# A dm step moved between two matmul halves, two loads issued later, and a table load moved, in a fused transformer-block backward kernel

## The chip, the cores and the metric

The kernel runs on one core of one Trainium2 chip. The metric is the device time of one execution in microseconds. Before the change it was run five times; the median is 819.18 us, the lowest 818.51, the highest 819.75. One more execution was taken with the hardware profiler.

## The reference

The kernel computes one transformer block and all of its gradients. x is 2048 x 640 in bf16, with 32 heads of 20 columns; the FFN is 1728 wide.

```python
def _A_ref(x, wqkv, wo):                      # linear attention
    qkv = (x @ wqkv) split into q, k, v per head
    phi = lambda t: jnp.where(t > 0, t + 1, jnp.exp(t)) + 1e-6
    pq, pk = phi(q), phi(k)
    kv = jnp.einsum("bhsd,bhse->bhde", pk, v)
    z = jnp.einsum("bhsd->bhd", pk)
    num = jnp.einsum("bhqd,bhde->bhqe", pq, kv)
    den = jnp.einsum("bhqd,bhd->bhq", pq, z)[..., None] + 1e-6
    return merge_heads(num / den) @ wo
def _B_ref(x, w_gate, w_up, w_down):          # SwiGLU
    return (_silu(x @ w_gate) * (x @ w_up)) @ w_down
h = x + _A_ref(_layernorm(x), A_wqkv, A_wo)
h2 = h + _B_ref(_layernorm(h), B_w_gate, B_w_up, B_w_down)
# outputs: h2, and by jax.vjp with grad_out the gradients of
# A_x, A_wqkv, A_wo, B_w_gate, B_w_up, B_w_down
```

## The kernel before

The 2048 rows are cut into 16 tiles of 128 rows (ST = 16), the 640 columns into 5 blocks of 128 (DT = 5). A product with 640 output columns is done as two halves of 320 columns (NCH), each of 5 matmuls, in the two banks of one PSUM buffer. There are four such buffers (`mm`). The stages follow one another on TensorE:

1. **Start and the k and q products** (0 to 55 us). `warm(31)` issues 31 small matmuls of the identity (ps_warm) while x arrives. Then tile 0 is centred on VectorE, transposed on TensorE (ps_t), copied to SBUF, eight more warm matmuls follow, and the products ps_kq begin.
2. **Attention summaries** (55 to 98 us). Y = xn^T pk (ps_y), the block-diagonal KV, and W2 = KV applied to wo (ps_w2t). Five pieces of W2T are written to SBUF by ScalarE, and each is transposed by an SP DMA (L524) into W2, which lies in the tile named wvo. Piece i gives the 128 columns i of W2. `normalise` runs on VectorE, four tiles at a time, and `tr_pqs` transposes its result into pqsT.
3. **dm steps.** `dm_steps` is a generator of 24 steps. One step multiplies dh2T (grad_out transposed) with a part of w_down for two row tiles: 10 matmuls (ps_dm, L396) and a ScalarE copy (L410); for the last eight steps also a store (scr_dm). They need nothing from attention, and `dm(n)` places n of them in other work: four among ps_y, five around W2, and one behind each of tiles 0 to 14 in the next loop.
4. **The attention loop** (98 to 148 us). For tile t: ps_a = pqsT[t] x W2 (10 matmuls in two halves by `mm_row`), VectorE adds x (xr), takes the statistics (mv2), GpSimd forms rstd (L139, L140). Two tiles later h1 is stored by a DMA on ScalarE's queue (scr_h, L554), VectorE writes hn (L555), and an SP DMA transposes it into hnT (L557).
5. **The FFN in four groups of columns** (148 to 456 us; 448, 448, 448, 384). For each pair of tiles TensorE computes pg (gate) and pu (up), 10 matmuls each; ScalarE makes two sigmoids and two copies (L604 to L607); VectorE makes seven products (L613), among them m_s (the product that the down projection's gradient reads) and dd (gradients of gate and up). dd is transposed by SP DMAs into three rotating `stg` tiles (L616) and stored by GpSimd DMAs (scr_dT, L617). After the eight pairs of a group come the weight gradients `dw` (ps_dw, L652). The first of them multiplies dh2 (grad_out itself, the tile shown as dh in the profile) with m_s, taking tiles 14 and 15 last; its results, dwev, are stored by GpSimd DMAs (L656).
6. **The backward pass through FFN, attention and both layer norms, and the output h2** (456 to 816 us).

The order on TensorE, VectorE and SP is written out by hand in stages 2 to 4; in stage 5 only SP's is, and ScalarE's, VectorE's and GpSimd's instructions are placed by a scheduler. DMAs go out on the queues of SP, ScalarE and GpSimd (POOL), each in order: an issue that waits holds up what is queued behind it.

What the change touches: dh2 is loaded in four quarters of four row tiles each (640 KB each) by GpSimd's queue (L563). Its buffer was pqsT's, so the loads can start when the last ps_a is done. The FFN's gate and up weights of a group are one tile `wgu` of two buffers, loaded on SP's queue (L185, L186); groups 0 and 1 are asked for ahead of the loop, the buffer of group 1 being free after the last dm step. `wait_for(on, dmas)` makes each of a list of DMAs wait for one instruction. The sigmoid's function table is loaded (ACT_TABLE_LOAD) where ScalarE first meets a sigmoid, in the first pair of group 0. `t` in the FFN loop steps by two, so t = 2 is the second pair.

Of the kernel before, what the change touches and what calls it, by code (L numbers as in the profile page):

```python
# [8 lines left out]
FP32 = mybir.dt.float32  # L9
BF16 = mybir.dt.bfloat16  # L10
ALU = mybir.AluOpType
ACT = mybir.ActivationFunctionType
# [3 lines left out]
P = 128  # L16
# [4 lines left out]
def kernel(  # L21
# [8 lines left out]
    nc = tc.nc  # L30
# [4 lines left out]
    DT = D // P  # L35
    NCH = [(0, 320), (320, 640)]
# [287 lines left out]
    with tc.manual_schedule(engines={EngineType.PE, EngineType.DVE, EngineType.Activation, EngineType.Pool}):  # L324

        ps = mm("ps_warm")

        def warm(n):
            for _ in range(n):
                nc.tensor.matmul(ps[:, 0, :P], lhsT=ident[:], rhs=ident[:], start=True, stop=True)  # L330

        def copies(t, eng_copy):
            for sl, src in ln1_tr(t):
                c = eng_copy(out=xnT[:, t, sl], in_=src)
                if t == 0 and sl.start == 0:
                    wait_for(c, load_3())

        def copy1(t):
            (nc.vector.tensor_copy if t in BY_V else nc.scalar.copy)(out=xnT[:, t], in_=ln1_tr1(t))

        warm(31)
        ln1_stats(0)
        ln1_centre(0, 0, 3 * P)
        ln1_centre(0, 3 * P, D)
        copies(0, nc.scalar.copy)
        warm(8)
        ln1_stats(1)
        ln1_centre(1)
        kq_mm(0, 0, lambda: copies(1, nc.vector.tensor_copy), PIECES)
        ln1_stats(2)  # L350
        ln1_centre(2)
        kq_mm(1, 0, None, PIECES)
        ln1_stats(3)
        kq_mm(0, 1, lambda: copy1(2), PIECES)
        phi(0, 0)
        ln1_xn(3)
        kq_mm(1, 1)
        for t in range(2, ST):
            if t == 2:
                ln1_stats(4)  # L360
            if t > 3 and t + 3 < ST:
                ln1_stats(t + 3)
            kq_mm(t, 0, (lambda: copy1(t + 1)) if t + 1 < ST else None)
            if t == 2:
                ln1_stats(5)
            if t == 3:
                ln1_stats(6)
            if t == ST - 1:
                phi(0, t - 1, 1)
            kq_mm(t, 1)  # L370
            if t == 3:
                phi(1, 0)
            elif t == ST - 1:
                phi(0, t, 1)
                phi(1, t - 3)
                phi(1, t - 1)
            elif t > 3:
                phi(t % 2, t - 2 - t % 2)
            if t + 2 < ST:
                ln1_xn(t + 2)  # L380
            if ST - NC - 1 <= t < ST - 1:
                ln1_xn(t - ST + NC + 1)
# [34 lines left out]
    def dm(n):  # L417
        for _ in range(n):
            next(dms, None)
# [41 lines left out]
    with tc.manual_schedule(engines={EngineType.PE, EngineType.DVE, EngineType.SP}):  # L461
        yk = strips.tile([P, DT * D + HG * P], BF16, name="yk", tag="S")
        Yt = yk[:, :DT * D].rearrange("p (k n) -> p k n", k=DT)
        KVT = yk[:, DT * D:].rearrange("p (j c) -> p j c", j=HG)
        zs = [wk("zs"), wk("zl")]

        def z_sum():
            ps = mm("ps_z")
            for ci, (n0, n1) in enumerate(NCH):
                for t in range(ST):  # L470
                    q = t % 4 * H
                    nc.tensor.matmul(ps[q:q + H, ci, :320], lhsT=ones[:, :H], rhs=pk[:, t, n0:n1],
                                     start=(t < 4), stop=(t >= ST - 4))
            nc.scalar.copy(out=half(zs[0][:]), in_=row(ps))
            nc.vector.tensor_tensor(out=half(zs[1][:]), in0=row(ps), in1=half(zs[0][:]), op=ALU.subtract)
            nc.vector.memset(KVT, 0.0)

        for i in range(DT):
            ps = mm("ps_y")
            for ci, (n0, n1) in enumerate(NCH):  # L480
                for t in range(ST):
                    nc.tensor.matmul(ps[:, ci, :320], lhsT=xn[:, t, i * P:(i + 1) * P], rhs=pk[:, t, n0:n1],  # L482
                                     start=(t == 0), stop=(t == ST - 1))
                if (i, ci) == (0, 0):
                    z_sum()
            nc.scalar.copy(out=half(Yt[:, i, :]), in_=row(ps))
            if i == 0:
                ps_z = mm("ps_zb")
                mm_row(ps_z, lambda k: ones32[:], lambda k, n0, n1: zs[k][:, n0:n1], 2)
                nc.scalar.copy(out=half(zb[:]), in_=row(ps_z))  # L490
                masks()
            if 0 < i < 4:
                dm(1)
        dm(1)
        for t in (0, 4):
            normalise(t)
            tr_pqs(t)
        for t in range(6):
            load_xr(t)
        nc.sync.dma_start(out=mat_v(scr_Yt), in_=Yt)  # L500
        def kv_blocks(dst, name, lhs, rhs):
            for js in ((0,), (1, 2), (3, 4), (5,)):
                h0, h1 = HC[js[0]]
                ps = mm(name)
                for c, j in enumerate(js):
                    for i in range(DT):
                        nc.tensor.matmul(ps[:, c, :h1 - h0], lhsT=lhs(i, OH[j], OH[j] + P),
                                         rhs=rhs(i, OH[j] + h0, OH[j] + h1), start=(i == 0), stop=(i == DT - 1))
                n = len(js)
                nc.vector.tensor_tensor(out=dst[:, js[0]:js[0] + n, h0:h1], in0=ps[:, :n, :h1 - h0],  # L510
                                        in1=head_mask(js[0], h1 - h0).unsqueeze(1).to_broadcast([P, n, h1 - h0]), op=ALU.mult)

        kv_blocks(KVT, "ps_kvt", lambda i, a, b: wv[:, i, a:b], lambda i, a, b: Yt[:, i, a:b])

        W2T = wv
        W2 = wo6[:, 0:5]
        dm(1)
        for i in range(DT):
            if i % 2 == 0 and i > 0:
                dm(1)  # L520
            ps = mm("ps_w2t")
            mm_heads(ps, lambda j: wo6[:, j, i * P:(i + 1) * P], lambda j, a, b: KVT[:, j, a:b])
            nc.scalar.copy(out=half(W2T[:, i, :]), in_=row(ps))
            nc.sync.dma_start_transpose(out=W2[:, :, i * P:(i + 1) * P], in_=W2T[:, i, :])  # L524
        for t in (8, 12):
            normalise(t)
            tr_pqs(t)
        dm(2)

        hn = big.tile([P, ST, D], BF16, name="hn", tag="B")  # L530
        hnT = big.tile([P, DT, S], BF16, name="hnT", tag="B")
        h1s = {}
        for t in range(ST + 2):
            if t < ST:
                xr = xrs.pop(t)
                ps = mm("ps_a")
                mm_row(ps, lambda i: pqsT[:, i, t * P:(t + 1) * P], lambda i, n0, n1: W2[:, i, n0:n1], DT)
                nc.vector.tensor_tensor(out=half(xr[:]), in0=row(ps), in1=half(xr[:]), op=ALU.add)
                mv = small.tile([P, 4, 2], FP32, name="mv2", tag="mv2")
                ln_stats(xr[:], mv[:, 0, :])  # L540
                ln_rstd(mv, rstd2, t, 1)
                h1s[t] = (xr, mv)
                dm(1)
            if t > 2:
                load_xr(t + 3)
            u = t - 2
            if u < 0:
                continue
            if u == 0:
                nc.sync.dma_start(out=scr_KVT.rearrange("(j p) c -> p j c", p=P), in_=KVT)  # L550
            if u == 2:
                nc.sync.dma_start(out=mat_v(scr_W2T), in_=W2T)
            h1, mv = h1s.pop(u)
            nc.scalar.dma_start(out=scr_h1_v[:, u, :], in_=h1[:])  # L554
            nc.vector.tensor_scalar(out=hn[:, u, :], in0=h1[:], scalar1=mv[:, 0, 0:1],  # L555
                                    scalar2=rstd2[:, u:u + 1], op0=ALU.subtract, op1=ALU.mult)
            nc.sync.dma_start_transpose(out=hnT[:, :, u * P:(u + 1) * P], in_=hn[:, u, :])  # L557


    with tc.manual_schedule(engines={EngineType.SP}):  # L560
        dh2 = big.tile([P, ST, D], BF16, name="dh2", tag="B")
        for c in range(4):
            nc.gpsimd.dma_start(out=dh2[:, c * 4:(c + 1) * 4, :], in_=go_v[:, c * 4:(c + 1) * 4, :])  # L563

        wgT = {}
        wgu = {0: load_wgu(0), 1: load_wgu(1)}

        def tr_wgT(g):
            k0, r0 = divmod(KO[g], 14)
# [4 lines left out]
        for g in range(4):  # L574
# [4 lines left out]
            for t in range(0, ST, 2):  # L579
# [21 lines left out]
                nsg = fw("nsg")[:, :, :w]  # L601
                u = fw("u")[:, :, :w]

                nc.scalar.activation(out=dg, in_=pg[:, :, :w], func=ACT.Sigmoid)  # L604
                nc.scalar.activation(out=nsg, in_=pg[:, :, :w], func=ACT.Sigmoid, scale=-1.0)
                nc.scalar.copy(out=m, in_=pg[:, :, :w])
                nc.scalar.copy(out=u, in_=pu[:, :, :w])  # L607
# [426 lines left out]
```

## Time and profile before

| | |
|---|---|
| median of five runs | 819.18 us (818.51 to 819.75) |
| profiled execution | 820.71 us, its span 818.70 us |
| TensorE matmuls | 811.5 us busy, 5534 instructions |
| VectorE, ScalarE, GpSimd | 443.0, 288.2 and 192.4 us busy |
| TensorE clock granted | 1.00 in the mean |
| mean DMA traffic | 194 GB/s, 158.61 MB moved |
| the dm group ps_dm | 47.0 us, 240 matmuls of 448 or 384 columns |

The span runs from the first to the last instruction of the profile; the 2.01 us between it and the execution's own time lie around it. PE stands for TensorE's matmuls, PEld for its weight loads, DVE for VectorE, ACT for ScalarE, POOL for GpSimd; SPq, ACTq and POOLq are DMA issues. A line of a timeline gives the start in us, the length in us, engine, source line, operation, output and inputs, and how many instructions were merged; in brackets stands how long the engine had been idle and what ended that. Lengths of merged matmuls include the drain of the last one, so that starts are the better measure of pitch. A line of the waits gives who waited for whom: us in total, times, longest.

### The profile page before, as it was taken

What the parts mean: (1) busy time and instruction counts of PE and PEld (TensorE: products, weight loads), DVE (VectorE), ACT (ScalarE), POOL (GpSimd) and SP (SyncE); (2) the same over time, 40 slices, a digit from 0 to 9 for tenths busy, and PEclk for the clock granted to TensorE, in tenths of its full rate; (3) what the DMA queues carried; (4) which work ended last, traced back from release to release, by engine and by line L of the source; (5) the groups of instructions that cost most, each with busy time, mean ns of one, the idle gap of its engine ahead of it and who ended that gap; (6) DMA issues with size and microseconds to landing.
All of it is one profiled execution on the core that took longest, in us unless ns stands there. A gap on an engine that the chain in (4) does not pass through costs nothing.

```text
span 818.7 us, 13969 instructions
## 1 busy us (share of the span) xinstructions
PE 811.5 (99%) x5534; PEld 521.9 (64%) x5534; DVE 443.0 (54%) x849; ACT 288.2 (35%) x405; POOL 192.4 (23%) x350
## 2 busy tenths in 40 slices
PE   8999999999999999999999999999999999999998
PEld 6776566545555555555566677777777777777675
DVE  7878787791077018810660147787793366631212
ACT  6982422770184126500741122322322133322010
POOL 3420022222312312221124511211220111112330
PEclk9999999999999999999999999999999999999999
DMA  9994699998559996995498757976498999999952
GB/s 302 189 357 88 166 197 273 263 226 191 159 130 196 218 219 145 199 247 115 101 241 170 261 134 218 221 203 180 111 240 169 161 173 178 169 199 263 242 165 72
DMA packets 278321, 158.61 MB, mean 194 GB/s; under 512 B 235052, under 2 KB 264877, under 8 KB 278256
## 3 DMA queue, kind: packets, MB, share of 16 engines
q1 hardware_dynamic: 251696, 82.12, 52.9%
q0 software_dynamic: 17744, 64.45, 26.0%
q10 hardware_dynamic: 8816, 11.16, 4.7%
q8 instruction: 43, 0.70, 0.4%
q14 instruction: 22, 0.18, 0.1%
HBM read 47.68 MB, written 53.66 MB: 124 GB/s over the span
## 4 chain that ended last, share of the span: by engine, by line
PE 94%; DVE 4%; DMA 1%; ACT 1%; issue 0%; ACTq 0%; DVEq 0%
PE ps_dw L652 21%; PE ps_dhn L109 14%; PE ps_dxn L904 8%; PE ps_o L966 7%; PE ps_kq L302 5%; PE ps_dwqk L109 5%; PE pu L588 5%; PE pg L583 5%; PE ps_dm L396 5%; PE ps_y L482 3%; PE ps_dp L109 3%; PE ps_dk L109 3%; PE ps_gt L711 3%; PE ps_a L109 3%; PE pdm L396 2%; DVE m_s L613 1%
## 5 line engine op out<-in xcount | busy, mean ns | idle before, releaser
L109 PE MATMUL ps_dhn<-wgT,cols 128*128 128x320 bf16 x864 | 119.5, 299 | 0.0
L652 PE MATMUL ps_dw<-dd,hn 128*128 128x448 bf16 (+1 forms) x640 | 118.8, 346 | 0.0
L109 PEld LDWEIGHTS <-cols 128*128 128x128 bf16 x864 | 84.5, 98 | 32.9
L652 PEld LDWEIGHTS <-hn 128*128 128x128 bf16 x640 | 62.6, 98 | 54.2
L654 DVE CAST dwev<-ps_dw 128x896 bf16<-128x896 f32 (+3 forms) x12 | 10.9, 906 | 122.9 <-PE ps_dw L652 122.9
L654 ACT CAST dwev<-ps_dw 128x896 bf16<-128x896 f32 (+1 forms) x20 | 17.6, 878 | 161.9 <-PE ps_dw L652 140.3
L617 POOL DMA_DIRECT2D scr_dT<-stg x64 | 34.7, 542 | 168.3 <-DMA stg<-dd 162.6
L147 DVE CUSTOM_DVE_ANT_0 lb_a<-lb_dy,hn 128x640 bf16<-128x640 bf16 x32 | 26.4, 825 | 75.1 <-ACT lb_dy L145 75.1
L583 PE MATMUL pg<-wgu,hnT 128*128 128x448 bf16 (+1 forms) x320 | 63.6, 346 | 0.0
L588 PE MATMUL pu<-wgu,hnT 128*128 128x448 bf16 (+1 forms) x320 | 63.6, 346 | 0.0
L652 PE MATMUL ps_dw<-m_s,dh 128*128 128x448 bf16 (+1 forms) x320 | 60.7, 346 | 0.7 <-DVE m_s L613 0.5
L966 PE MATMUL ps_o<-wd,mT 128*128 128x320 bf16 (+3 forms) x462 | 61.1, 295 | 0.0
L904 PEld LDWEIGHTS <-ring 128*128 128x128 bf16 x480 | 47.0, 98 | 18.2
L966 PEld LDWEIGHTS <-mT 128*128 128x128 bf16 (+1 forms) x462 | 41.8, 97 | 17.4 <-issue 2.6
L904 PE MATMUL ps_dxn<-wqkvT,ring 128*128 128x320 bf16 x320 | 51.3, 299 | 0.0
L652 PEld LDWEIGHTS <-dh 128*128 128x128 bf16 x320 | 31.3, 98 | 28.1 <-issue 1.2
L588 PEld LDWEIGHTS <-hnT 128*128 128x128 bf16 x320 | 31.3, 98 | 27.1
L583 PEld LDWEIGHTS <-hnT 128*128 128x128 bf16 x320 | 31.3, 98 | 27.0
L396 PE MATMUL ps_dm<-wdT,dh2T 128*128 128x448 bf16 (+1 forms) x240 | 47.0, 344 | 0.0
L396 PEld LDWEIGHTS <-dh2T 128*128 128x128 bf16 x320 | 31.0, 98 | 24.8
L302 PE MATMUL ps_kq<-wqk,xnT 128*128 128x320 bf16 x320 | 46.6, 300 | 0.0
L145 ACT ACTIVATE lb_dy<-ps_dhn,rstd 128x640 bf16<-128x640 f32 x16 | 12.7, 793 | 84.8 <-PE ps_dhn L109 84.8
(166 smaller groups left out, 1278.3 us busy)
## 6 DMA issues: line engine op xcount, KB each, us to landing
scr_dT<-stg POOLq DMA_DIRECT2D x48, 224.0 KB, 3.5
cols<-scr_dT POOLq DMA_DIRECT2D x6, 1728.0 KB, 8.2
scr_m<-m_s POOLq DMA_DIRECT2D x12, 448.0 KB, 4.4
cols<-scr_dT ACTq DMA_DIRECT2D x2, 1728.0 KB, 10.3
out_dram<-dwev POOLq DMA_DIRECT2D x30, 112.0 KB, 2.2
scr_dT<-stg POOLq DMA_DIRECT2D x16, 192.0 KB, 2.9
scr_pk<-pk SPq DMA_DIRECT2D x4, 640.0 KB, 8.2
scr_xnT<-xnT SPq DMA_DIRECT2D x4, 640.0 KB, 8.3
```

Source lines behind the costliest of these rows:

```text
L109: nc.tensor.matmul(ps[:, ci, :320], lhsT=lhs(k), rhs=rhs(k, *NCH[ci]), start=(start and k == 0), stop=(stop and k == n - 1))
L147: nc.vector.tensor_tensor_reduce(out=a[:], in0=dy[:], in1=xhat, scale=1.0, scalar=0.0, op0=ALU.mult, op1=ALU.add, accum_out=sums[:, 1:2])
L302: nc.tensor.matmul(ps[:, ci, :320], lhsT=xnT[:, t, k, :], rhs=wqk[:, k, w0 + n0:w0 + n1], start=(k == 0), stop=(k == DT - 1))
L396: nc.tensor.matmul(ps[:, c, :w], lhsT=dh2T[:, kt, (t + c) * P:(t + c + 1) * P], rhs=wdT[:, kt, o:o + w], start=(kt == 0), stop=(kt == DT - 1))
L482: nc.tensor.matmul(ps[:, ci, :320], lhsT=xn[:, t, i * P:(i + 1) * P], rhs=pk[:, t, n0:n1], start=(t == 0), stop=(t == ST - 1))
L583: nc.tensor.matmul(pg[:, c, :w], lhsT=hnT[:, kt, (t + c) * P:(t + c + 1) * P], rhs=wg[:, kt, 0:w], start=(kt == 0), stop=(kt == DT - 1))
L588: nc.tensor.matmul(pu[:, c, :w], lhsT=hnT[:, kt, (t + c) * P:(t + c + 1) * P], rhs=wg[:, kt, w:2 * w], start=(kt == 0), stop=(kt == DT - 1))
L617: nc.gpsimd.dma_start(out=scr_dT[t + c, :, KO[g]:KO[g] + GK[g], :], in_=stg[:, :GK[g], :])
L652: nc.tensor.matmul(ps[:, c, :w], lhsT=lhs(t), rhs=rhs(t), start=(t == 0), stop=(t == ST - 1))
L654: last = copy(out=ev[:, :len(parts), :w], in_=ps[:, :len(parts), :w])
L904: nc.tensor.matmul(ps[:, ci, :320], lhsT=lhs[:, i, :], rhs=rhs[:, i, n0:n1], start=(k == 0 and i == 0), stop=(k == 2 and i == DT - 1))
L966: nc.tensor.matmul(po(t, ci), lhsT=mTs[t // 4][r, t % 4, j, :], rhs=wd[r, j, n0:n1], start=(t, ci) not in opened, stop=last)
```

## The change

Four edits. Six more warm matmuls at the very start (37 instead of 31). In the attention loop the two halves of tile 0 are written out, and its dm step stands between them instead of behind them. Ahead of the DMA that stores KVT, in the loop's third pass, a sigmoid of one column goes to ScalarE, into a tile `sg` that nothing reads; the sigmoid table is loaded there. The four loads of dh2 now wait for the first sigmoid of the second pair of group 0, and the weights of group 1 are loaded at that place of the program instead of ahead of the loop. The instruction order that comes out is otherwise the same, except that on GpSimd's queue the last quarter of dh2 stands behind two scr_dT stores, that the last rstd of the attention loop stands ahead of the dh2 loads, and that VectorE's product `a` stands one place later in four pairs of group 0.

```diff
@@ -338,7 +338,7 @@
         def copy1(t):
             (nc.vector.tensor_copy if t in BY_V else nc.scalar.copy)(out=xnT[:, t], in_=ln1_tr1(t))
 
-        warm(31)
+        warm(37)
         ln1_stats(0)
         ln1_centre(0, 0, 3 * P)
         ln1_centre(0, 3 * P, D)
@@ -534,19 +534,27 @@
             if t < ST:
                 xr = xrs.pop(t)
                 ps = mm("ps_a")
-                mm_row(ps, lambda i: pqsT[:, i, t * P:(t + 1) * P], lambda i, n0, n1: W2[:, i, n0:n1], DT)
+                for ci, (n0, n1) in enumerate(NCH):
+                    for i in range(DT):
+                        nc.tensor.matmul(ps[:, ci, :320], lhsT=pqsT[:, i, t * P:(t + 1) * P], rhs=W2[:, i, n0:n1],
+                                         start=(i == 0), stop=(i == DT - 1))
+                    if t == 0 and ci == 0:
+                        dm(1)
                 nc.vector.tensor_tensor(out=half(xr[:]), in0=row(ps), in1=half(xr[:]), op=ALU.add)
                 mv = small.tile([P, 4, 2], FP32, name="mv2", tag="mv2")
                 ln_stats(xr[:], mv[:, 0, :])
                 ln_rstd(mv, rstd2, t, 1)
                 h1s[t] = (xr, mv)
-                dm(1)
+                if t > 0:
+                    dm(1)
             if t > 2:
                 load_xr(t + 3)
             u = t - 2
             if u < 0:
                 continue
             if u == 0:
+                nc.scalar.activation(out=small.tile([P, 1], FP32, name="sg", tag="sg", bufs=1)[:], in_=h1s[0][1][:, 0, 0:1],
+                                     func=ACT.Sigmoid)
                 nc.sync.dma_start(out=scr_KVT.rearrange("(j p) c -> p j c", p=P), in_=KVT)
             if u == 2:
                 nc.sync.dma_start(out=mat_v(scr_W2T), in_=W2T)
@@ -559,11 +567,13 @@
 
     with tc.manual_schedule(engines={EngineType.SP}):
         dh2 = big.tile([P, ST, D], BF16, name="dh2", tag="B")
-        for c in range(4):
-            nc.gpsimd.dma_start(out=dh2[:, c * 4:(c + 1) * 4, :], in_=go_v[:, c * 4:(c + 1) * 4, :])
+
+        def load_dh2():
+            for c in range(4):
+                yield nc.gpsimd.dma_start(out=dh2[:, c * 4:(c + 1) * 4, :], in_=go_v[:, c * 4:(c + 1) * 4, :])
 
         wgT = {}
-        wgu = {0: load_wgu(0), 1: load_wgu(1)}
+        wgu = {0: load_wgu(0)}
 
         def tr_wgT(g):
             k0, r0 = divmod(KO[g], 14)
@@ -601,7 +611,10 @@
                 nsg = fw("nsg")[:, :, :w]
                 u = fw("u")[:, :, :w]
 
-                nc.scalar.activation(out=dg, in_=pg[:, :, :w], func=ACT.Sigmoid)
+                sig = nc.scalar.activation(out=dg, in_=pg[:, :, :w], func=ACT.Sigmoid)
+                if g == 0 and t == 2:
+                    wait_for(sig, load_dh2())
+                    wgu[1] = load_wgu(1)
                 nc.scalar.activation(out=nsg, in_=pg[:, :, :w], func=ACT.Sigmoid, scale=-1.0)
                 nc.scalar.copy(out=m, in_=pg[:, :, :w])
                 nc.scalar.copy(out=u, in_=pu[:, :, :w])
```

## The prediction

> **What bounds the kernel now.** The page comes first.
>
> ```profile
> PE 811.5 (99%) x5534; PEld 521.9 (64%) x5534; DVE 443.0 (54%) x849; ACT 288.2 (35%) x405; POOL 192.4 (23%) x350
> PE 94%; DVE 4%; DMA 1%; ACT 1%; issue 0%; ACTq 0%; DVEq 0%
> ```
>
> TensorE is busy 811.5 of 818.7 us and carries 94% of the chain that ended last. The change removes no matmul, so all it can win is idle TensorE, 7.2 us in all, and slow matmuls at the start. The waits of TensorE say where 3.6 us of that idle time lies (most of the rest is the tail after the last matmul, which the change does not touch):
>
> ```profile
> PE ps_warm L330 <- POOL ident masks.py:199: 1.4, 1, 1.4
> PE ps_a L109 <- DMA wvo<-wvo: 1.0, 1, 1.0
> PE ps_t L286 <- DVE xn L275: 0.7, 1, 0.7
> PE ps_dw L652 <- DVE m_s L613: 0.5, 1, 0.5
> ```
>
> Lines two to four are the three places that the change touches. The timeline shows each; its first two columns are start and length. First the attention tile:
>
> ```profile
> 94.86 3.94 PE L396 MATMUL ps_dm<-wdT,dh2T 128*128 128x448 bf16 x20
> 98.64 0.84 PE L109 MATMUL ps_a<-wvo,pqsT 128*128 128x320 bf16 x5
> 100.51 0.85 PE L109 MATMUL ps_a<-wvo,pqsT 128*128 128x320 bf16 x5 [1.03 <-DMA wvo<-wvo]
> 101.20 2.06 PE L396 MATMUL ps_dm<-wdT,dh2T 128*128 128x448 bf16 x10
> 103.09 1.52 PE L109 MATMUL ps_a<-wvo,pqsT 128*128 128x320 bf16 x10
> ```
>
> The first half of tile 0 runs at once, since it needs three of the five transposed blocks of W2. The second half stands still for the last blocks, and the dm step that needs none of them is queued behind it.
>
> Next the start of the FFN and the end of its first group:
>
> ```profile
> 148.65 1.00 POOL L563 DMA_DIRECT2D dh<-in_grad_out_dram  x1 [0.58 <-issue]
> 148.87 2.07 ACTq L554 DMA_DIRECT2D scr_h<-xr  x1
> 149.71 2.05 PE L588 MATMUL pu<-wgu,hnT 128*128 128x448 bf16 x10
> 150.97 1.28 ACT L604 ACT_TABLE_LOAD   x1 [3.52 <-DVE hn L555]
> 152.27 0.92 ACT L604 ACTIVATE dd<-pg 128x896 bf16<-128x896 f32 x1
> 154.82 0.62 DVE L613 TENSOR_TENSOR m_s<-m_s,dd 128x896 bf16<-128x896 bf16 x1 [2.56 <-ACT m_s L606]
> ...
> 178.08 2.43 PE L652 MATMUL ps_dw<-m_s,dh 128*128 128x448 bf16 x12
> 180.37 0.62 DVE L613 TENSOR_TENSOR m_s<-m_s,u 128x896 bf16<-128x896 bf16 x1
> 181.04 4.25 PE L652 MATMUL ps_dw<-m_s,dh 128*128 128x448 bf16 x20 [0.52 <-DVE m_s L613]
> 183.71 0.61 DVE L613 TENSOR_TENSOR m_s<-m_s,u 128x896 bf16<-128x896 bf16 x1
> ```
>
> The first gate product is complete when pu starts, 149.71, but ScalarE reads it only at 152.27: a DMA issue held it to 150.94 (2.07 us where the same issue takes 0.33 in the loop) and the table load for 1.28 more. VectorE therefore starts at 154.82 and never catches up: its seven products per pair of tiles take 7 x 0.535 = 3.75 us, TensorE's pair 2 x 1.89 = 3.78. That lag is paid at the end, where the weight gradient stops twice for m_s.
>
> Last the cold start:
>
> ```profile
> 1.42 3.49 PE L330 MATMUL ps_warm<-ident 128*128 128x128 bf16 x31 [1.42 <-POOL ident masks.py:199]
> 5.56 0.71 PE L286 MATMUL ps_t<-ident,xn 128*128 128x128 bf16 x5 [0.65 <-DVE xn L275]
> 6.07 1.06 PE L330 MATMUL ps_warm<-ident 128*128 128x128 bf16 x8
> 6.92 1.23 PE L302 MATMUL ps_kq<-wqk,xnT 128*128 128x320 bf16 x6
> ```
>
> Until about 7.7 us everything is slow (five transposes 0.71 us; the next five take 0.44).
>
> **The change part by part**, in the times of the profiled execution.
>
> *A, the dm step between the halves.* At full pitch, 2.72 / 20 = 0.136 us for a 320-column matmul, the first half would end at 98.64 + 5 x 0.136 = 99.32. The second starts at 100.51: 1.19 us lost by pitch, 1.03 by the wait row (modelled ends make the difference). The dm step is 10 matmuls, 1.89 us. Put at 99.32 it ends at 101.21, after the last block of W2 has landed (97.80 + 2.66 = 100.46). The second half then starts at 101.21 and tile 1 at 101.89 instead of 103.09. Gain 1.03 to 1.19; I take 1.2. Would it be given back? Queued behind are the next tiles and dm steps, which need PSUM buffers. In the compiled order tile 2 and tile 3 wait for ScalarE's copies of dm, and the dm step of tile 2 for VectorE's addition of tile 0. VectorE is in the normalisation until 105.02, so that addition still ends at 104.93 + 0.82 = 105.75. Moved up 1.2 us, that dm step starts at 106.50: 0.75 to spare. Without this cover up to 0.75 to 1.2 would return.
>
> *B, the table load in the attention loop.* A one-column activation, and with it the 1.28 us load, now stands on ScalarE's queue behind the dm copy of tile 1, ahead of two scr_h issues and the next dm copy. ScalarE has idle time of 2.35 and 2.42 us before these copies, so it costs at most a copy some tenths late, with more than 2 us until its buffer is wanted. The table row is followed at once by the activation (150.97 + 1.28 = 152.25), so 1.28 is its price here. The Trainium skill, ScalarE: Activation LUTs, section What ACT_TABLE_LOAD costs, puts a switch at about 1.28 us of load plus 1.38 us of drain. By that figure the move would free 2.66 us of ScalarE; the trace shows no drain behind the load, and the sum would not change by either.
>
> *C, dh2 and the second FFN weights later.* Gone from 146.6 to 153 are two weight loads on SP's queue and four dh2 issues on POOL's, which also stood ahead of the last row's rstd (hn of tile 15 waited 1.14 us). ScalarE's scr_h issue should fall back from 2.07 to 0.33. So ScalarE can take the first gate product at about 149.9, VectorE starts about 2.4 us earlier (154.82 to 152.45; its last hn is done by 151.5). What that is worth on TensorE: twelve matmuls from 178.08 at 0.189 end at 180.35, and the twenty others at 184.13; the next group began at 185.13. That is 1.0 us lost. To win all of it m_s must come 0.64 us earlier for the first stop (180.99 against 180.35) and 0.96 for the second (184.33 against 183.37). The 2.4 us cover it, and so would the 1.28 us of the table load alone. Gain 0.52 (the wait row) to 1.0; I take 1.0.
>
> What the move adds: dh2 now waits for the second sigmoid, about 154.5 (its gate product ends at 153.49). On POOL's queue three quarters are issued, then two scr_dT stores that wait for their transposes, then the last quarter, then all other stores. On SP the second weights stand behind two transposes. The second weights are needed only at 224.6, the first three quarters of dh2 at 178.08; both have over 10 us. The last quarter is needed at 180.35, which is the danger (first rival). POOL's stores behind it free the dwev buffers; six of them at one per 6.05 us from 185.4 give until about 221, and POOL was through with the first group's stores at 211 to 216.
>
> *D, six more warm matmuls.* At 3.49 / 31 = 0.113 us they take 0.68, where TensorE idled for 0.65: the transposes start at most 0.1 late. If the clock came up sooner, the five transposes (0.27), six kq (0.4) and the second warm group would run at full rate: at most about 0.8. The row for this start shows the clock up at 7.7 in spite of the gap. The Trainium skill, TensorE: Matmul & The Clock Gate, Part 1, says that the rise depends on a free-running window and not on a count of matmuls, and advises against fitting one; that speaks against D, and by it the sum would hold zero for D. I take 0.1, with ends -0.1 and 0.8, near zero because the gap did not hold the clock down in the one row there is.
>
> **Sum:** 1.2 + 1.0 + 0.1 = 2.3 us, ends 1.45 and 3.0. The profiled execution took 820.71 us (span 818.70 and 2.01 around it); it becomes 818.4. It lay 1.5 above the median of the runs, 819.18, and I carry the difference over: 819.18 - 2.3 = 816.9. A change of 0.2%, 1.64 us, is about what a measurement of this kernel can tell from no change.
>
> **The rivals.** *Slower: the last quarter of dh2 is late.* The chain: dd of the first pair is ready at 156.4; two transposes, the second's landing, two scr_dT issues (0.55), the quarter's issue (0.8) and its landing. With quiet rows (transposes issue in 1.26 and land in 3.6, a 640 KB load 5.7): 156.5 + 1.3 + 3.6 + 0.6 + 0.8 + 5.7 = 168.5. With the crowded rows of 146 to 165 (3.5, 8.9, and 9.2 for dh2): 179.5. With the longest (6.2, 13.0, 11.0): 188.1. Needed at 180.35. Only three quarters crowd the queues now, so I expect about 174. At the longest TensorE stands 7.7 us, net 7.7 - 2.3 = 5.4 slower, 824.6. It decides from a landing at 184.3 on (3.9 us, which is 2.3 and 1.64). Chance 0.12.
>
> *Half of it.* Either A returns at a PSUM buffer, leaving 1.1, or VectorE is still late at m_s, because its pitch leaves it only 0.03 us per pair to catch up, leaving 1.3: 818.1 or 817.9. For it: the narrow 0.75 of A. Against: the covers above. Chance 0.15, mostly within 0.2%.
>
> *Nothing moves, or something unseen is late* (DMA engines are full from 148 to 186): 0.05.
>
> **How the numbers follow.** The forecast has 0.68; its own range is 816.2 to 817.7. With the half gain at 818.1 the range holds over 0.8: 816.0 to 818.3. Faster by over 0.2% (below 817.54) is most of the forecast and a little of the half gain, 0.69; within 0.2%, 0.18; slower 0.13.
>
> **What would show it.** Right: no wait of ps_a on wvo and none of ps_dw on m_s; the table load near 107; the first sigmoid within 0.4 us of the first gate product; dh2 landed by 176. Wrong: a wait of ps_dw on a DMA near 180, a wait of ps_dm on VectorE near 106, or the start moving by more than 0.8 us.

## The result, and the profile after

The changed kernel takes 817.6 us, the median of 32 runs (817.12 to 819.18). The kernel before, run beside it, took 819.36 us (57 runs; its first five, shown above, have 819.18). The ratio is 0.9977, with a 95% interval of 0.9972 to 0.9983: 1.4 to 2.3 us less, 1.9 at the middle. The forecast was faster by 2.3 us, 816.9, with a range of 816.0 to 818.3.

The profiled execution of after took 818.04 us with a span of 816.1; that of before 820.71 and 818.70. The two profiles therefore differ by 2.67 us, more than the medians do (2.59 of span and 0.08 around it). That difference comes back below.

The page of after, beside the two lines shown of before:

```profile
PE 811.7 (99%) x5540; PEld 522.5 (64%) x5540; DVE 442.9 (54%) x849; ACT 288.9 (35%) x406; POOL 193.3 (24%) x350
PE 99%; DMA 1%; SPq 0%; POOL 0%; issue 0%; DVE 0%; POOLq 0%
```

Busy TensorE time is the same (811.7 with six more small matmuls), and the chain that ended last is now TensorE for 99%, not 94%: what has gone is idle time of TensorE. Of the four waits of TensorE in the profile of before, one is left in that of after, the wait for the identity at the very start:

```profile
PE ps_warm L330 <- POOL ident masks.py:199: 1.4, 1, 1.4
```

The timeline of after shows the three places. The attention tile first; columns as before (start, length, engine, what, how many, and in brackets the idle time and its releaser):

```profile
98.52 0.84 PE L539 MATMUL ps_a<-wvo,pqsT 128*128 128x320 bf16 x5
99.20 2.06 PE L396 MATMUL ps_dm<-wdT,dh2T 128*128 128x448 bf16 x10
101.09 2.20 PE L539 MATMUL ps_a<-wvo,pqsT 128*128 128x320 bf16 x15
104.82 0.82 DVE L543 TENSOR_TENSOR xr<-ps_a,xr 128x640 bf16<-128x640 f32 x1
106.38 2.06 PE L396 MATMUL ps_dm<-wdT,dh2T 128*128 128x448 bf16 x10
106.96 1.28 ACT L556 ACT_TABLE_LOAD   x1
108.25 0.20 ACT L556 ACTIVATE sg<-mv 128x1 f32<-128x1 f32 x1
```

The dm step stands between the halves without a gap. The fifteen ps_a that follow are the second half of tile 0 and all of tile 1, so tile 1 starts at 101.09 + 5 x 0.136 = 101.77, which is 3.25 us behind the first half; before it was 103.09 - 98.64 = 4.45. Part A won 1.20 us. VectorE's addition ends at 105.64, and the dm step that waits for it starts at 106.38, 0.74 later. The table load stands in ScalarE's idle time near 107.

Then the FFN's start and the end of its first group:

```profile
147.55 0.33 ACTq L562 DMA_DIRECT2D scr_h<-xr  x1
148.39 2.05 PE L598 MATMUL pu<-wgu,hnT 128*128 128x448 bf16 x10
148.59 0.92 ACT L614 ACTIVATE dd<-pg 128x896 bf16<-128x896 f32 x1 [2.45 <-PE pg L593]
151.15 0.63 DVE L626 TENSOR_TENSOR m_s<-m_s,dd 128x896 bf16<-128x896 bf16 x1 [0.89 <-ACT m_s L619]
153.60 2.50 POOL L573 DMA_DIRECT2D dh<-in_grad_out_dram  x3 [3.82 <-ACT dd L614]
168.65 1.16 POOL L630 DMA_DIRECT2D scr_dT<-stg  x2 [12.54 <-DMA stg<-dd]
169.80 0.76 POOL L573 DMA_DIRECT2D dh<-in_grad_out_dram  x1
176.76 6.22 PE L665 MATMUL ps_dw<-m_s,dh 128*128 128x448 bf16 x32
182.82 7.35 PE L665 MATMUL ps_dw<-dd,hn 128*128 128x448 bf16 x38
```

The scr_h issue is back at 0.33 us. The sigmoid now waits for pg itself and follows it by 0.2 us (pu starts at 148.39, when pg is complete). The 32 matmuls of dh2 run without a stop. From the first pg of the FFN (146.50, 147.82 before) to the next dw group it is 36.32 us, where it was 37.31: 0.99 us won. The last quarter of dh2 is the narrow place: issued at 169.80, it landed 8.2 us later, at 178.0, and the matmuls that read it come at 176.76 + 12 x 0.189 = 179.03. There was 1.1 us to spare.

At the start the second kq group begins at 8.15 us, 8.27 before: 0.12 for part D. Of the three gains, 2.31 us up to 182.8, 0.22 is lost between 614 and 750 us at one wait, of ps_dxn for a transposed piece of dq (0.4 us); the rest of the span's 2.6 lies in a tail of 2.9 instead of 3.4 us after the last matmul, which comes back below.

### The profile page after: what moved, and what is told of

Same layout as the page of the kernel before. It is cut to its first block, busy times and chain, and to the rows that moved or that the text cites. A ratio compares the mean times of both kernels' runs of the same rounds, so it can differ in the third digit from the quotient of the medians.

```text
span 816.1 us, 13979 instructions
## 1 busy us (share of the span) xinstructions
PE 811.7 (99%) x5540; PEld 522.5 (64%) x5540; DVE 442.9 (54%) x849; ACT 288.9 (35%) x406; POOL 193.3 (24%) x350
## 4 chain that ended last, share of the span: by engine, by line
PE 99%; DMA 1%; SPq 0%; POOL 0%; issue 0%; DVE 0%; POOLq 0%
PE ps_dw L665 21%; PE ps_dhn L109 14%; PE ps_dxn L917 7%; PE ps_o L979 7%; PE pu L598 7%; PE pg L593 7%; PE ps_kq L302 5%; PE ps_dwqk L109 5%; PE ps_dm L396 5%; PE ps_y L482 3%; PE ps_dp L109 3%; PE ps_gt L724 3%; PE ps_a L539 3%; PE ps_dk L109 2%; PE pdm L396 2%; DMA ring<-dq 1%
```

## The experiments

The theory was the prediction's: A gains what the wait for W2 cost, B and C gain what the stops for m_s cost, D about 0.1. The rivals were that only one of B and C does the work, that the warm matmuls matter more than their 0.1, and that the gains are those of one profile and not of most executions. Each kernel was also profiled once; the figures from the traces are gathered behind the single parts.

**A alone.**

```diff
-                mm_row(ps, lambda i: pqsT[:, i, t * P:(t + 1) * P], lambda i, n0, n1: W2[:, i, n0:n1], DT)
+                for ci, (n0, n1) in enumerate(NCH):
+                    for i in range(DT):
+                        nc.tensor.matmul(ps[:, ci, :320], ...)
+                    if t == 0 and ci == 0:
+                        dm(1)
...
-                dm(1)
+                if t > 0:
+                    dm(1)
```

> The dm step between the halves of tile 0, alone. Theory: 1.2 us faster (ratio 0.9985); no wait of ps_a on wvo; tile 1 starts 3.25 us after tile 0 instead of 4.45; the stops of ps_dw for m_s stay as before. Rival (the gain returns at a PSUM buffer, since VectorE frees tile 0's only near 105.8): 0.4 us or less, with a wait of ps_dm or ps_a near 106.

Measured: 818.76 us, ratio 0.9992 (0.9984 to 1.0001). There is no wait of ps_a in its trace, and the second half starts 2.57 us behind the first (0.68 of matmuls and 1.89 of the dm step). But it shows no stop for m_s either, though the table is loaded late and dh2 early, as before. Its timeline says why:

```profile
146.72 0.60 ACTq L560 DMA_DIRECT2D scr_h<-xr  x1
147.35 1.28 ACT L610 ACT_TABLE_LOAD   x1 [2.05 <-DVE xr L543]
148.65 0.92 ACT L610 ACTIVATE dd<-pg 128x896 bf16<-128x896 f32 x1
```

The scr_h issue took 0.60 us and not 2.07, so ScalarE reached the first gate product 1.10 us after it was complete, not 2.56. The profiled execution, 818.03 us, was the lowest of this kernel's 11 runs.

**B alone.**

```diff
+                nc.scalar.activation(out=small.tile([P, 1], FP32, name="sg", ...)[:],
+                                     in_=h1s[0][1][:, 0, 0:1], func=ACT.Sigmoid)
```

> The sigmoid table loaded in the attention loop, alone. Theory: the first sigmoid comes 1.27 us earlier (at about 151.0), which is more than the 0.96 that the end of group 0 needs; the two stops for m_s go; 1.0 us faster (0.9988). The slow scr_h issue stays. Rival (VectorE is held by the last rstd behind the dh2 issues, so that an earlier ScalarE is worth little): a stop for m_s stays, 0.5 us or less.

Measured: 818.73 us, ratio 0.9994 (0.9985 to 1.0002). The issue took 0.91 us and the sigmoid still followed its gate product by 0.2: with the table in place there is room for a long issue. No stop for m_s. The wait for W2 is there (0.7), and 1.2 us were lost at the start, where wqk came late.

**C alone.**

```diff
-        wgu = {0: load_wgu(0), 1: load_wgu(1)}
+        wgu = {0: load_wgu(0)}
...
+                if g == 0 and t == 2:
+                    wait_for(sig, load_dh2())
+                    wgu[1] = load_wgu(1)
```

> dh2 and the second FFN weights later, alone. Theory: the scr_h issue falls from 2.07 to 0.33 us, the first sigmoid comes 1.7 us earlier although the table load is still in front of it, the stops for m_s go; 1.0 us faster (0.9988). Rival (the later loads cost elsewhere, by late transposes or a late last quarter): same or slower.

Measured: 818.52 us, ratio 0.9988 (0.9979 to 0.9997). The issue took 0.33 us; the table load then made the sigmoid 0.82 us late, and TensorE did not stop for m_s. The wait for W2 is 1.0 us.

**D alone.**

```diff
-        warm(31)
+        warm(37)
```

> 37 warm matmuls, alone. Theory: 0.1 us faster, not to be told from no change (0.9996 to 1.0002). Rival (the closed gap brings the clock up a window earlier): 0.4 to 0.8 us, ratio 0.9990 to 0.9995, and a first ps_t group of 0.44 us.

Measured: 819.3 us, ratio 1.0002 (0.9994 to 1.0011): nothing. The trace of this kernel, which differs from before by six matmuls at the very start, has no stop for m_s, and the wait for W2 is down to a fifth:

```profile
147.46 0.33 ACTq L554 DMA_DIRECT2D scr_h<-xr  x1
...
149.11 0.92 ACT L604 ACTIVATE dd<-pg 128x896 bf16<-128x896 f32 x1
```

```profile
PE ps_a L109 <- DMA wvo<-wvo: 0.2, 1, 0.2
```

If six matmuls at the very start took away these waits 100 us on, the kernel would be 1.8 us faster than the first profile; its ratio leaves room for 0.5 at most. So the waits seem to differ from one execution to the next, and the profiled one, 818.38 us, was the lowest of the 12 runs. This made the third rival, one profile against most executions, the one to follow.

**The change without one part, and B with C.** Without B (A, C and D), without C (A, B and D), and B and C alone; the edits are those shown, left out or kept.

> The whole change without the table load in the attention loop. Theory (the moved loads alone already bring the first sigmoid early enough, the two parts pay for the same stop): no stop for m_s, time as of the whole change, ratio 0.9975 to 0.9980. Rival (each part has a gain of its own, about 0.5 us for the table): 0.9983.

> The whole change without the later loads of dh2 and of the second FFN weights. Theory: the table part alone takes the stop away, ratio 0.9975 to 0.9980. Rival (the later loads have a gain of their own, 0.6 to 0.8 us): 0.9985 to 0.9987, and the profile shows where: a stop for m_s or another one in the first group.

> Table load and later loads together, without the halves and without the warm matmuls. Theory as predicted: 1.0 us faster, 0.9988, the wait of ps_a on wvo still there. Rival (the profiled execution of before was a dear one, and the stop for m_s is missing in many executions): 0.3 to 0.6 us, 0.9993 to 0.9996.

Measured: without B 817.71 us, ratio 0.9983 (0.9974 to 0.9992); without C 818.45, 0.9989 (0.9980 to 0.9999); B and C alone 818.66, 0.9990 (0.9974 to 1.0006). None of the three traces has a stop for m_s. In that without C the sigmoid is 0.2 us behind its product although the loads are early. So no stop was left in a trace with only one of B and C. The times are not equal, though. Both kernels were expected at 0.9975 to 0.9980; without B it is nearly so, without C not, and there the rival's figure, a gain of the later loads of their own, is the nearer one. Run side by side, nine of the eleven runs without B took less than 818.0 us, and one of the eleven without C. What the later loads gain beyond the stop is not in the first group; it comes back below. B and C alone still wait 0.6 for W2.

**The slower rival, forced.** The loads of dh2 wait for the sigmoid two pairs of tiles later.

```diff
-                if g == 0 and t == 2:
+                if g == 0 and t == 6:
```

> The whole change with dh2 and the second weights tied to the fourth pair's sigmoid instead of the second's. The last quarter of dh2 landed at 178.0 after the change, wanted at 179.0; here it is issued behind six scr_dT stores, at 172 to 174, and lands near 181. Theory of the late quarter: a wait of ps_dw on a DMA of 1 to 3 us, time 818.6 to 820.6, ratio 0.999 to 1.002. Rival (there is room, the queues are quieter then): no wait, 0.9977.

Measured: 830.29 us (825.61 to 831.91), ratio 1.0123 (1.0095 to 1.0151). Waits and timeline of this kernel:

```profile
PE ps_dw L665 <- DMA dh<-in_grad_out_dram: 10.6, 2, 10.0
```

```profile
177.83 0.76 POOL L573 DMA_DIRECT2D dh<-in_grad_out_dram  x1
...
190.18 6.64 PE L665 MATMUL ps_dw<-m_s,dh 128*128 128x448 bf16 x20 [9.98 <-DMA dh<-in_grad_out_dram]
196.66 12.27 PE L665 MATMUL ps_dw<-dd,hn 128*128 128x448 bf16 x64
```

The weight gradient waits twice for dh2, the longer time, 9.98 us, for the last quarter, which is issued at 177.83 behind a scr_dT store that had waited 5.2 us for its transpose, and lands 12.3 us later. The mechanism and the place are the rival's. The wait is longer than the 1 to 3 us that were expected of this run, by the issue (172 to 174 was expected) and by the landing. The wait also has a second price: the granted clock falls to half at 182.0 us and is full again at 195.7, so that the 20 matmuls behind the wait, which take 20 x 0.189 = 3.78 us elsewhere, reach the next group only after 196.66 - 190.18 = 6.48 us.

**The kernel before, twice more, for its trace.** No edit.

> The kernel before, profiled a second time. Theory (the first profile was a dear execution): the last scr_h issue takes less than 1 us, the first sigmoid begins less than 1.6 us after the first gate product is complete, there is no stop for m_s, and the span is near 817.4 instead of 818.7. Rival (the stop is there every time, as the prediction took it): two stops for m_s, 1.0 us, span above 818.2.

> The kernel before, profiled a third time: the same two expectations as for the second. Should one of the two show the stop and the other not, it comes in a part of the executions.

Measured: 819.62 and 820.31 us, one execution each, both above the median like the first. The second is nearer the rival (issue 1.92 us, stop 0.85), though its span is 817.6; the third lies between. Of the second a line of the waits, and of the second and then the third the timeline at the FFN's start:

```profile
PE ps_dw L652 <- DVE m_s L613: 0.4, 1, 0.4
```

```profile
147.93 1.92 ACTq L554 DMA_DIRECT2D scr_h<-xr  x1
...
151.18 0.92 ACT L604 ACTIVATE dd<-pg 128x896 bf16<-128x896 f32 x1
```

```profile
149.03 1.30 ACTq L554 DMA_DIRECT2D scr_h<-xr  x1
151.66 0.92 ACT L604 ACTIVATE dd<-pg 128x896 bf16<-128x896 f32 x1
```

The five traces with the table late and the loads early now make a row, ordered by the length of that one scr_h issue. The sigmoid's lateness is its start less that of pu. The loss is the time from the first ps_dw to the next dw group, less 32 x 0.189 = 6.05:

| trace | scr_h issue | sigmoid after pg | lost at m_s |
|---|---|---|---|
| before | 2.07 | 2.56 | 1.00 |
| before, second | 1.92 | 2.42 | 0.85 |
| before, third | 1.30 | 1.80 | 0.22 |
| A alone | 0.60 | 1.10 | 0 |
| D alone | 0.33 | 0.82 | 0 |

The mean loss is 0.41 us. The prediction held that an earlier m_s by 0.96 us would win all of it, that is, a sigmoid at most 2.56 - 0.96 = 1.60 us late; the row lies on both sides of that and agrees (1.80 - 0.22 = 1.58).

The wait for W2, by pitch, in the seven traces without part A: 1.19 (before), 0.88, 0.81 (before, second and third), 0.89 (B), 1.12 (C), 0.35 (D), 0.80 (B and C); the mean is 0.86. In the traces with part A it is 0.

**The change with dh2 one pair earlier**, to see whether the narrow margin costs time.

```diff
-                if g == 0 and t == 2:
+                if g == 0 and t == 0:
```

> The whole change with dh2 and the second weights tied to the first pair's sigmoid. All four quarters of dh2 then stand ahead of the scr_dT stores. Theory: the last quarter lands 8 us or more before it is wanted, the median is that of the change (0.9977), and the dearest tenth of the executions (818.7 and more with the change) is cheaper, if a late quarter makes them. Rival (the loads crowd the last transposes and scr_h again): 0.5 to 0.8 us slower than the change, 0.9985.

Measured: 817.96 us, ratio 0.9979 (0.9967 to 0.9991); one of its 12 runs took 820.24. All four issues follow one another from 149.95 us on and land in 6.6 to 10.0 us, far ahead of 179. No wait is left but the first. It is not faster than the change, so the narrow margin costs nothing that can be seen; that the dearest executions become cheaper is not shown either.

**The change again**, on the same chip.

> The whole change again, beside the run before. Both theories: 0.9977; the last quarter of dh2 lands between 172 and 179 with no wait of ps_dw.

Measured: 817.54 us, ratio 0.9981 (0.9969 to 0.9992); one of its 11 runs took 820.8. The profile has the one wait at the start. The last quarter of dh2 was issued at 165.61 and landed at 173.9, 4.9 us ahead of its use, where the first profile of this kernel has 1.1.

## Why the prediction was right, and where its sizes were off

The direction held and the time lies in the range, and the waits that A, B and C were made for are gone. That the sum of 2.3 us came so near the measured 1.9 is in part luck: by the mean over the traces its terms were 1.0 us too high, and some 0.6 us came from a place that it had put at nothing.

**A** was forecast at 1.2 us with ends of 1.03 and 1.19, and between the two profiles it measures 1.20. Its cover held as worked out: 0.74 us from VectorE's addition to the dm step that waits for it (0.75 forecast), and no dm copy late behind the table load. The first "half of it" rival, that A returns at a PSUM buffer, is out. The size was that of one execution: over seven traces the wait for W2 costs 0.35 to 1.19 us, 0.86 in the mean. Alone, A gave 0.7 us (0.0008 of 819), with an interval from -0.1 to 1.3.

**B and C** were forecast at 1.0 us, and between the two profiles they measure 0.99, with VectorE's first product 2.35 us earlier in its place (2.4 forecast). The second "half of it" rival, a VectorE that is still late, is out: 0.2 us behind the gate product was enough every time. But the stop that they remove was 1.00, 0.85, 0.22, 0 and 0 in five traces, 0.41 in the mean. The prediction said that either edit would cover the stop. In none of the eight traces with one or both of them (dh2 two pairs later left aside) is there a stop for m_s, but A alone and D alone had none either. What speaks for C is that the issue took 0.53 us at most in all traces with dh2 later; for B the longest issue in a trace was 0.91 us, so that B covers an issue of 2 us (2.56 - 1.28 = 1.28 us late, below 1.58) is argued from the row and not shown.

**D** was forecast at 0.1, with ends of -0.1 and 0.8. It is worth nothing that can be seen: alone 1.0002, and the first half of tile 0 starts at 98.32 us in the mean of seven traces with 31 warm matmuls and at 98.37 in seven with 37. What moves the start is something else: the first transposes begin at 5.0 to 5.6 us, wqk comes up to 1.2 us late, and the record of the full clock begins at 4.2 to 7.4 us from the span's start with 31 warm matmuls (six traces; a seventh has no record) and at 4.5 to 7.2 with 37 (seven). The Trainium skill, TensorE: Matmul & The Clock Gate, Part 1, says that the rise follows a free-running window of time and not a count of matmuls; the runs agree, and its zero for D was the better term. It gives some 0.5 us to either side for the rise; the traces here lie 3.2 us apart.

**The first step that failed** is "I carry the difference over". It set the sum, read from an execution of 820.71 us, against the median of 819.18, as if the 1.5 us between them had nothing to do with the terms. But that profile was the dearest of the three of this kernel in just these places: it has the longest wait for W2 of seven traces and the longest stop for m_s of five. With the means in place of the single values the sum is 0.86 + 0.41 + 0 = 1.27 us, which would have given 819.18 - 1.27 = 817.9, 0.3 above the median of after where the forecast is 0.7 below it.

**The second step that failed** is the tail, "which the change does not touch". The last group of matmuls ends at 815.31 us in the profile of before and at 813.22 in that of after, 3.39 and 2.89 us before the end of the span:

```profile
807.52 7.79 PE L966 MATMUL ps_o<-wd,mT 128*128 128x320 bf16 x70
805.43 7.79 PE L979 MATMUL ps_o<-wd,mT 128*128 128x320 bf16 x70
```

All fourteen traces divide the same way. "Tied to" means the pair whose sigmoid the loads of dh2 wait for; the last column is the start of the first 8 KB packet on the instruction queue (q14) behind the issue of the last output store.

| loads of dh2 | traces | tail | time around the span | landing of the last store | q14 packet |
|---|---|---|---|---|---|
| early | 7 | 3.23 to 3.60 | 2.00 to 2.01 | 1.89 to 2.27 | 0.66 to 0.91 |
| tied to the first pair | 1 | 3.14 | 1.91 | 1.81 | 0.67 |
| tied to the second or fourth | 6 | 2.78 to 2.91 | 1.83 to 1.93 | 1.45 to 1.46 | 2.84 to 2.95 |

The instructions of the tail and their times up to the last store are the same. Where the packet starts while the store is under way, the store lands late; that the packet delays it is inferred from this row, and why part C moved the packet is not shown. The gain is 0.5 us of tail and 0.1 around the span, and it has nothing to do with a wait for m_s. With it the sum is 0.86 + 0.41 + 0 + 0.6 = 1.87 us. By the same sizes A alone should gain 0.9, B alone 0.4, C alone 1.0, the change without B 1.9 and without C 1.3; measured are 0.7, 0.5, 1.0, 1.4 and 0.9, and each size lies within its interval.

**What stays open** is the size of the stop for m_s. Its mean is 0.41 us over five traces, but 0.69 over the three of the kernel before, which all lie above its median, and 0 over those of A alone and D alone, which are the lowest of their kernels' runs. Small waits come and go besides, such as 0.3 us of ps_dm for ScalarE's dmst in the third profile of before. No run tells these apart.

**The slower rival** did not come, but it was closer than its chance of 0.12 sounds. "dh2 landed by 176" missed: in the first profile of after it landed at 178.0. The estimate of about 174 fits the second profile (173.9). The chain is the one written down; the step that was too short in the first profile is the transposes of dd, which landed 12.6 and 13.2 us after their issue (8.6 and 9.3 in the second; the crowded row had 8.9). In the three other kernels with dh2 at the second pair the last quarter landed at 172.5, 173.1 and 176.8 us, 2.7 us or more ahead of its use. At two pairs later the cliff is there, 10.6 us of waiting.

**Nothing moves** is out: the interval does not reach 1.

## What to carry to other kernels

A wait of a microsecond that hangs on a DMA's landing or a queue's issue time differs from one execution to the next; take its size from three or four profiles of the kernel before, not from one, and least of all from an execution that lies above the median. Two edits that each remove the same lateness don't add up: work out the lateness from which the stop begins, and credit the gain once. When a load is moved later, write down the chain that it then waits for, with its longest landing, and look at the margin in more than one profile, because a few tiles on can be a cliff. Compare the tail of the program in every trace too, and credit a gain to a mechanism only where it is found: here 0.6 of 1.9 us lay in a place that no edit was made for.

## What the runs showed of the hardware

- The last scr_h store before the FFN took 0.33, 0.38, 0.60, 0.91, 1.30, 1.92 and 2.07 us to issue in the seven traces with dh2 and the second weights loaded early, and 0.33 us, once 0.53, in the seven with dh2 later (in six of them the second weights too). What sets it within the first seven is not shown.
- The two transposing DMAs of dd took 12.6 and 13.2 us to land in the first profile of after, and 8.6 and 9.3 in the second, while three quarters of dh2 (1.9 MB) were in flight; between 262 and 269 us the same kind landed in 2.9 to 4.7 us in these two profiles. The last quarter of dh2 itself landed in 6.5 to 8.3 us in the five traces with dh2 at the second pair, and in 12.3 us two pairs later.
- The table load took 1.28 us in every trace, and the activation followed it at once (106.96 + 1.28 = 108.24, start at 108.25). The Trainium skill, ScalarE: Activation LUTs, section What ACT_TABLE_LOAD costs, adds a drain of about 1.38 us to each switch; no trace here shows one behind the load, and in the profile of after none shows ahead of it: the copy before it ended at 106.94 us.
- With the same start of the program (31 warm matmuls) the record of the full clock began at 7.4, 4.2 and 6.1 us in the three profiles of before and at 4.9 and 5.1 us with A and with B alone; with 37 at 7.2 and 6.1 us in the two profiles of after and at 5.8 with D alone.
- In the kernel with dh2 two pairs later TensorE waited 9.98 us for dh2, until 190.18 us; the granted clock was at half from 182.0 to 195.7 us.
- The last output store, the same in every trace, landed 1.45 or 1.46 us after its issue in six traces and 1.81 to 2.27 us after it in eight, in which an 8 KB packet of the instruction queue started 0.66 to 0.91 us behind that issue.
